# Three projection tiles begun with plain fp32 products of unsplit data, the early transfers timed anew, and a new order for the strips

## The chip, the cores and the metric

The kernel runs on one core of a Trainium2 chip. The metric is the device time of one execution in microseconds (us). The engines are TensorE (PE in the profile, its weight loads PEld), VectorE (DVE), ScalarE (ACT), GpSimd (POOL) and SyncE (SP). SP, ACT and POOL issue DMAs, each through a queue of its own.

## The reference

```python
x = A_x                                     # [1, 2048, 448]
g = sigmoid((x * gate_w).sum(-1, keepdims=True))
q, k, v = split(x @ wqkv)                   # 16 heads of 28
p = softmax(q @ k.T * 28 ** -0.5)           # 2048 x 2048 for each head
a = (p @ v) @ wo
b = gelu(layernorm(x) @ w1 + b1) @ w2 + b2  # 448 -> 1792 -> 448
return g * a + (1 - g) * b
```

Everything is fp32. The host only lays data out: x transposed with its 448 rows padded to four blocks of 128 (`xt`), and the weights cut into 128-wide tiles in the same four blocks.

## The kernel before, in words

**Split products.** A product of fp32 data is made of three or two products of split data. ACT rounds a raw tile to `fp32r` (the high part: `x_high`, `mixed_high`), DVE or POOL subtracts it from the raw tile (the low part: `x_low`, `mixed_low`), and PE adds high x high, high x low and low x high in one PSUM bank. A tile `QK(c, m)` is the 128 projection columns `m` of the 512 tokens of chunk `c`; `m` 0 to 6 covers queries and keys.

**Head.** The first three tiles, (0,0), (0,3) and (0,4), are made with the full 128-row array (L1011). SP loads weights and x chunk by chunk into eight raw slots (L984, L986); a slot is loaded again when both parts were made. Eight filler products (L991) stand before the first real one, four more between the first ones.

**Strips.** After that PE runs as four 32-row strips that work side by side on different matmuls (L549). A planner, `Strips.run`, is run while the program is written: it keeps a clock for each strip and for DVE, ACT, POOL and the DMA, and writes out the next matmul of the strip whose clock is lowest. So the order of PE is fixed; on the chip PE works it off in order. Three kinds of work share the strips: projections (`QK`, `Val`), the MLP (`Up`, `Down`), and the **row maxima** (L212): q x k scores of one head, 512 wide, in bank 6 or 7, whose row maximum DVE reduces (L214). There are 1024 of these and they are needed before the softmax of their query block. Wherever a row maximum is ready the planner takes it, except at the steps in the list `PASSES`, where it takes other work. What isn't made in the strips is left for attention. A piece of work handed from one strip to another goes through a semaphore that SP raises (L590), in SP's own order.

**Early transfers.** The first projections go to DRAM (`qk`) through ACT's queue (L304) and come back, head by head, through POOL's queue into `qd` (L196) and `kd` (L186); the first row maximum needs them. Chunk 3 of x comes through POOL's queue before that (L632). Weight tiles 2 and 6 take the places of tiles 0 and 3 and are asked for when these are done (`PLACE`, `done`).

**Attention.** A *turn* is four score tiles (`turn_of`, 12 matmuls, L1227), exponentials on ACT (L1233), and four products with v for the turn before (L1293, plain fp32). Two pairs of banks take the scores, the third pair is `spare`; the spare pair of one turn is the first pair of the next. While row maxima are left, `lone` puts one into bank 6 at the turn's start and one into bank `spare` at its end. Once none is left, the turns take a shorter form with all banks in a ring (L1260, L1261). At the end `finish_last` and `put` scale and project the last block, and SP stores it (L1096).

## Time and profile before

| | |
|---|---|
| time, median of 3 runs (lowest to highest) | 1023.41 us (1023.4 to 1024.1) |
| the profiled execution: its time, its span | 1024.39 us, 1022.6 us |
| PE busy | 1014.5 us, 99% |
| DVE busy | 747.3 us, 73% |
| ACT busy | 666.4 us, 65% |
| POOL busy | 359.6 us, 35% |
| row maxima: matmuls (L212), reductions (L214) | 1024 of 426 ns, 1024 of 689 ns |
| granted PE clock | 1.00 |

The profile is of one execution. Its own time is 1.8 us above its span; what lies between is start and end, and no query shows it. PE counts as busy whenever any strip works, so 99% doesn't say that four strips are full. The duration of a matmul includes its way through the array; what one costs is the distance between the starts of two that follow each other. The text after an arrow in a row names what ended the idle time before it.

### The profile page before, as it was taken

The numbers are of one execution on the slowest core, as the hardware profiler recorded it, in microseconds if no ns is written. First come the engines' busy times: TensorE is split into PE (matmuls) and PEld (weight loads), VectorE is DVE, ScalarE is ACT, GpSimd is POOL, SyncE is SP. The second block draws the span as 40 slices with busy tenths as digits, with TensorE's granted clock in tenths as the row PEclk, the third lists the DMA queues.
The fourth block names the chain that finished last, engine by engine and source line by source line (L and its number), as shares of the span: only waits on it lengthen the run. The fifth ranks groups of instructions, "written<-read, shape, count | busy, mean of one in ns | idle before, by whom it ended". The sixth has DMA issues, their size and how long they took to land.

```text
span 1022.6 us, 30999 instructions
## 1 busy us (share of the span) xinstructions
PE 1014.5 (99%) x13159; PEld 672.9 (66%) x13159; DVE 747.3 (73%) x1178; ACT 666.4 (65%) x1059; POOL 359.6 (35%) x376
## 2 busy tenths in 40 slices
PE   9999999999999999999999999999999999999998
PEld 7899999999999999944444444444444444464555
DVE  4899998999999999966666666656666666644111
ACT  5225365034043044189999999999999999969664
POOL 4558578626335034151011001400111223455324
PEclk9999999999999999999999999999999999999999
DMA  7688543211110014261000100310002101021121
GB/s 239 193 246 272 190 121 102 84 59 53 35 41 12 9 42 100 47 164 32 12 17 27 41 14 17 103 46 12 17 28 62 54 12 58 21 78 36 55 64 56
DMA packets 49666, 73.42 MB, mean 72 GB/s; under 512 B 13780, under 2 KB 30804, under 8 KB 48700
## 3 DMA queue, kind: packets, MB, share of 16 engines
q1 hardware_dynamic: 37096, 42.76, 14.5%
q0 software_dynamic: 4368, 14.39, 4.9%
q10 hardware_dynamic: 8064, 14.29, 3.9%
q8 instruction: 103, 1.69, 0.7%
q14 instruction: 35, 0.29, 0.1%
HBM read 51.98 MB, written 19.31 MB: 70 GB/s over the span
## 4 chain that ended last, share of the span: by engine, by line
PE 97%; DMA 2%; ACT 0%; DVE 0%; POOL 0%; SPq 0%; issue 0%
PE bk L549 35%; PE bk L1293 25%; PE bk L1227 17%; PE bk L212 15%; PE bk L1088 1%; DMA qk<-qo 1%; PE bk L1090 1%; PE bk L1089 1%; PE bk L1011 1%; DMA first<-in_xt 0%; ACT qo L300 0%; DMA kd<-qk 0%; POOL qd L196 0%; ACT xh L103 0%; PE bk L991 0%
## 5 line engine op out<-in xcount | busy, mean ns | idle before, releaser
L214 DVE TENSOR_REDUCE mx<-bk 128x1 f32<-128x512 f32 x1024 | 683.6, 689 | 174.4 <-PE bk L212 152.0
L1233 ACT ACTIVATE p<-bk 128x512 f32<-128x512 f32 (+1 forms) x693 | 462.4, 741 | 39.7 <-PE bk L1227 13.6
L212 PE MATMUL bk<-kd,qd 28*128 28x512 f32 x1024 | 435.0, 426 | 1.4 <-DMA kd<-qk 1.4
L212 PEld LDWEIGHTS bk<-kd,qd 28*128 28x128 f32 x1024 | 186.1, 182 | 201.9 <-DVE mx L214 180.4
L549 PE MATMUL bk<-yh,w1f 32*128 32x512 f32 x1568 | 182.4, 391 | 0.0
L549 PE MATMUL bk<-yl,w1f 32*128 32x512 f32 x784 | 159.3, 390 | 0.0
L549 PEld LDWEIGHTS bk<-yh,w1f 32*128 32x128 f32 x1568 | 151.2, 183 | 0.6
L549 PE MATMUL bk<-w2h,hh 32*128 32x448 f32 x896 | 140.3, 364 | 0.0
L549 PE MATMUL bk<-w2l,hh 32*128 32x448 f32 x896 | 139.8, 363 | 0.0
L1293 PE MATMUL bk<-p,vb 128*32 128x512 f32 x1024 | 136.2, 604 | 0.1
L1128 POOL TENSOR_TENSOR ot<-ob,rc 128x512 f32<-128x512 f32 x12 | 15.4, 1285 | 343.3 <-DMA rc<-rls 312.1
L1293 PE MATMUL bk<-p,va 128*32 128x512 f32 x1016 | 135.4, 605 | 0.0
L369 POOL TENSOR_TENSOR hl<-h,hh 128x512 fp32r<-128x512 f32 x56 | 72.0, 1296 | 124.5 <-ACT hh L361 51.7
L549 PEld LDWEIGHTS bk<-w2h,hh 32*128 32x128 f32 x896 | 105.5, 183 | 0.2
L549 PEld LDWEIGHTS bk<-w2l,hh 32*128 32x128 f32 x896 | 105.3, 183 | 0.1
L549 PEld LDWEIGHTS bk<-yl,w1f 32*128 32x128 f32 x784 | 103.8, 183 | 0.1
L1227 PE MATMUL bk<-yh,ka 29*128 29x512 f32 x508 | 92.6, 470 | 0.0
L549 PE MATMUL bk<-w2h,hl 32*128 32x448 f32 x896 | 87.2, 362 | 0.0
L1227 PE MATMUL bk<-yh,kb 29*128 29x512 f32 x512 | 86.4, 476 | 0.0
L360 ACT ACTIVATE h<-bk,b1s 128x512 f32<-128x512 f32 x56 | 38.2, 683 | 68.7 <-PE bk L549 50.8
L1227 PE MATMUL bk<-yh,la 28*128 28x512 f32 x508 | 79.5, 393 | 0.0
L1227 PE MATMUL bk<-yl,ka 28*128 28x512 f32 x508 | 78.8, 390 | 0.0
(147 smaller groups left out, 1610.0 us busy)
## 6 DMA issues: line engine op xcount, KB each, us to landing
qk<-qo ACTq DMA_DIRECT2D x28, 256.0 KB
raw<-in_xt SPq DMA_DIRECT2D x20, 256.0 KB
vs<-vt ACTq DMA_DIRECT2D x16, 256.0 KB
rc<-rls SPq DMA_DIRECT2D x60, 64.0 KB
bxr<-in_xk POOLq DMA_DIRECT2D x8, 448.0 KB, 5.4
yl<-qk SPq DMA_DIRECT2D x64, 56.0 KB
acc<-gbs SPq DMA_DIRECT2D x16, 224.0 KB
out_y<-acc SPq DMA_DIRECT2D x16, 224.0 KB
```

The costliest lines, as they stand in the source:

```text
L212: nc.tensor.matmul(ps, self.qd[n % 2][r, i * P:(i + 1) * P], self.kd[r, k * 512:(k + 1) * 512], start=True, stop=True)
L214: nc.vector.reduce_max(self.mx[n % 2][:, j, i, k:k + 1], ps, axis=AX)
L360: nc.scalar.activation(h, bk[:, self.bank], AF.Gelu_apprx_tanh, bias=b1s[:, f:f + 1])
L369: nc.gpsimd.tensor_sub(hl[f], h, hh[f].bitcast(F32))
L549: mm = nc.tensor.matmul(bk[:, x.bank, :n], a, b, start=x.first, stop=(len(x.rem) == 1 and m == len(ops) - 1), skip_group_check=True)
L1011: nc.tensor.matmul(bk[:, first[k].bank], w, v, start=(o == (k, hi, 0)), stop=(o == (k, by, 3)), skip_group_check=True)
L1088: nc.tensor.matmul(po, h, woh[:, g], start=(g == 0), stop=False, skip_group_check=True)
L1089: nc.tensor.matmul(po, h, wol[:, g], start=False, stop=False, skip_group_check=True)
L1128: nc.gpsimd.tensor_mul(ot[g][:, c * CH:(c + 1) * CH], ob, rc)
L1227: nc.tensor.matmul(bk[:, b], w[r, ks], q[r], start=(p == 0), stop=(p == 2), skip_group_check=True)
L1233: nc.scalar.activation(t[:, i:e], bk[:, b + i:b + e], AF.Exp, scale=SCALE)
L1293: nc.tensor.matmul(bk[32 * j:32 * j + 32, 7], vg[n // NC][:, k, 32 * j:32 * j + 32], prob[4 * b + j], start=(k == 0), stop=(k == NT - 1), ...
```

## The change

The head's order becomes x, x, then the three weight tiles, then x again, so that the first raw x block is there first. ACT's queue loads the first 128 rows of the three weight tiles a second time, unsplit, into a buffer that is idle then (`early_w`). PE takes the first of the four row blocks of the three tiles as three plain fp32 products of raw data (L992 in the new kernel) in place of nine split ones; the four fillers between products go, the eight ahead stay. The other products of the head stand in a new order. The evictions of the three tiles stand before the split of weight tile 1 on ACT.

Of the early transfers, weight tiles 2 and 6 get places in `yh` and `yl`, which are idle until the MLP, and are asked for at a fixed point; the first load of `qd` and `kd` is planned one microsecond later, and POOL's issue of a block of `kd` is planned with 2.05 us in place of 0.6.

`PASSES` goes from 15 to 91 steps, and the banks are tried in another order. In attention a row maximum comes from the other two strips when the first two have none ready, both may stand at the turn's start, and every 24th turn has a third one in bank `spare + 1`. The three small DVE steps that make the gate go from turn 2 to turns 21, 22 and 23, one each. The last output tile is scaled and stored in two halves, by SP and by ACT.

```diff
@@ -83,7 +83,6 @@
     lasting = [raws.tile([P, CH], F32, name=f"raw{i}") for i in range(4)]
     passing = [pr.tile([P, CH], F32, name=f"first{i}") for i in range(4)]
     wq, xh, xl = {}, {}, {}
-    PLACE = {2: 0, 6: 3}
 
     def four(r):
         return r.rearrange("p (a b) -> p a b", b=P)
@@ -238,10 +237,10 @@
     nc.vector.memset(rowmax.kd[:, 0:CH].bitcast(F32), 0.0)
 
 
-    PASSES = (1195, 1746, 2729, 2778, 2911, 3059, 4477, 5337, 6201, 6646, 6792, 6828, 6838, 7051, 7243)
+    PASSES = (2, 15, 55, 79, 86, 95, 105, 302, 435, 518, 533, 593, 618, 644, 975, 993, 1186, 1301, 1312, 1349,
...
     HOP = 0.51
     SCORED = 16.0
-    BANKS = (2, 1, 4, 5, 3, 0)
+    BANKS = (1, 2, 4, 0, 5, 3)
     RATE = 230.0
     RM = 0.65
     handoff = mybir.DependencyInfo(mybir.DependencyClass.Sync, mybir.DependencyReason.DATA)
@@ -648,7 +647,7 @@
 
         st.at(st.act + 0.1, rest)
 
-    def want_x(st, c, t):
+    def want_x(st, c, t, **kw):
         def then(slot, end):
             st.feed.back(slot, end)
             st.xs[c] = st.xs.get(c, 0) + 1
@@ -656,7 +655,7 @@
                 st.xready[c] = end
 
         st.feed.add(xt[t, :, c * CH:(c + 1) * CH], 256, lambda r: two(
-            st, lambda: x_high(c, t, r), lambda: x_low(c, t, r), "dve", 0.85, lambda end: then(r, end)))
+            st, lambda: x_high(c, t, r), lambda: x_low(c, t, r), "dve", 0.85, lambda end: then(r, end)), **kw)
 
     def want_wq(st, m, **kw):
         def then(slot, end):
@@ -664,7 +663,10 @@
             st.wready[m] = end
 
         def use(r):
-            wq[m] = pw.tile([P, 7, P], F32R, name=f"wq{PLACE.get(m, m)}")
+            if m in (2, 6):
+                wq[m] = (yh, yl)[m == 2][:, 0:2].rearrange("p a b -> p (a b)")[:, 0:7 * P].rearrange("p (a b) -> p a b", b=P)
+            else:
+                wq[m] = pw.tile([P, 7, P], F32R, name=f"wq{m}")
             two(st, lambda: mixed_high(wq[m], r), lambda: mixed_low(wq[m], r, m % 2), "pool", 1.6, lambda end: then(r, end))
 
         st.feed.add(wqk[m], 256, use, **kw)
@@ -800,13 +802,6 @@
         n = st.did[type(x), x.c]
         if isinstance(x, QK):
             st.qks.add((x.c, x.i))
-            for old, new in ((0, 2), (3, 6)):
-                if new not in wq and new not in st.asked and all((c, old) in st.qks for c in range(NC)):
-                    st.asked.add(new)
-                    want_wq(st, new)
-                    st.feed.queue.insert(0, st.feed.queue.pop())
-                    st.clock = max(st.clock, now)
-                    st.feed.pump()
             if x.i in (3, 4) and all((x.c, m) in st.qks for m in (3, 4)):
                 keys(st, x.c, now + 5.0)
             if not st.keyed and all((c, m) in st.qks for c in range(NC) for m in (3, 4)):
@@ -834,7 +829,7 @@
                     st.use("pool", st.clock, 0.55)
                     st.get(st.pool, 56)
             rowmax.load_block(c, nc.gpsimd)
-            st.use("pool", st.clock, 0.6)
+            st.use("pool", st.clock, 2.05)
             st.at(st.get(st.pool, 230) + 1.0, landed)
 
         def landed():
@@ -867,10 +862,12 @@
         st.wready.update({0: 0.0, 3: 0.0, 4: 0.0})
         st.late, st.later, st.shifted, st.unshifted = False, [], None, []
         st.xs, st.wvn, st.stats, st.lns, st.go, st.yn = {}, 0, 0, {}, {0}, {}
-        keys(st, 0, 4.0)
+        keys(st, 0, 5.0)
         for t in range(4):
-            want_x(st, 3, t)
+            want_x(st, 3, t, after=2.5)
         want_wq(st, 5, after=9.0)
+        for m in (2, 6):
+            want_wq(st, m, after=28.0)
         for t in range(4):
             want_wv(st, t, after=42.0)
         for f in range(NW):
@@ -919,10 +916,9 @@
         loads[0].dma_start(qh[n % 3][DH:P:32].bitcast(F32),
                           ms[n][0:16].rearrange("(j i) b x -> j (i b x)", j=4))
 
-    def gates():
-        nc.vector.tensor_scalar_add(gate, gate, 1.0)
-        nc.vector.reciprocal(gate, gate)
-        nc.vector.tensor_scalar(ngate, gate, -1.0, 1.0, op0=OP.mult, op1=OP.add)
+    gates = (lambda: nc.vector.tensor_scalar_add(gate, gate, 1.0),
+             lambda: nc.vector.reciprocal(gate, gate),
+             lambda: nc.vector.tensor_scalar(ngate, gate, -1.0, 1.0, op0=OP.mult, op1=OP.add))
 
     def early(st, now):
 
@@ -975,48 +971,56 @@
 
     loads = [nc.gpsimd]
     strips = Strips([])
-    load = [("wq", 0), ("x", 0, 0), ("wq", 3), ("wq", 4)] + [("x", 0, t) for t in range(1, 4)]
+    load = [("x", 0, 0), ("x", 0, 1), ("wq", 0), ("wq", 3), ("wq", 4), ("x", 0, 2), ("x", 0, 3)]
     load += [("x", 1, t) for t in range(4)] + [("wq", 1)] + [("x", 2, t) for t in range(4)]
     slots = passing + lasting
+    first = [QK(0, m) for m in (0, 3, 4)]
+    for k, x in enumerate(first):
+        x.bank = BANKS[k]
+    early_w = bxr[1][:, 0, 0:3 * P].rearrange("p (k a) -> p k a", a=P)
+    nc.scalar.dma_start(early_w[:, 0], wqk[0][:, 0])
+    nc.scalar.dma_start(early_w[:, 1:3], wqk[3:5].rearrange("m p t a -> p m t a")[:, :, 0])
+
+    def warm(n):
+        for _ in range(n):
+            nc.tensor.matmul(bk[:, 7], rowmax.kd[:, 0:P], rowmax.kd[:, 0:CH], start=True, stop=True, skip_group_check=True)
+
+    warm(8)
     for i, key in enumerate(load):
+        if i == 8:
+            for k, x in enumerate(first):
+                nc.tensor.matmul(bk[:, x.bank], early_w[:, k], slots[0], start=True, stop=False, skip_group_check=True)
         r = slots[i % 8]
         if key[0] == "wq":
             nc.sync.dma_start(four(r), wqk[key[1]])
         else:
             nc.sync.dma_start(r, xt[key[2], :, key[1] * CH:(key[1] + 1) * CH])
-        if 3 <= i < 15:
+        if 3 <= i < 14:
             head_split(i - 3)
-    def warm(n):
-        for _ in range(n):
-            nc.tensor.matmul(bk[:, 7], rowmax.kd[:, 0:P], rowmax.kd[:, 0:CH], start=True, stop=True, skip_group_check=True)
-
-    strips.feed.slots = slots[:4]
+    strips.dve = 1.2
     schedule_head(strips)
-    first = [QK(0, m) for m in (0, 3, 4)]
     parts = [x.full() for x in first]
-    hi, lo, by = range(3)
-    order = [(0, hi, 0), (0, by, 0), (0, lo, 0), 2, (1, hi, 0), (1, by, 0), 1, (1, lo, 0), (2, hi, 0), (2, by, 0), 1,
-             (0, hi, 1), (0, lo, 1), (1, hi, 1), (1, lo, 1), (2, hi, 1), (2, lo, 0), (2, lo, 1), (0, by, 1), (1, by, 1), (2, by, 1)]
-    for t in (2, 3):
-        order += [(k, p, t) for p in (hi, lo, by) for k in range(3) if p != lo or t < 3]
-    warm(8)
-    for k, x in enumerate(first):
-        x.bank = BANKS[k]
-    for o in order:
-        if isinstance(o, int):
-            warm(o)
-            continue
-        k, p, t = o
+    hi, by, lo = range(3)
+    order = [(0, hi, 1), (1, hi, 1), (0, lo, 1), (1, lo, 1), (2, hi, 1), (2, lo, 1)] + [(k, hi, 2) for k in range(3)]
+    order += [(0, by, 1), (0, by, 2)] + [(k, p, t) for p, t in ((lo, 2), (hi, 3), (lo, 3)) for k in range(3)]
+    order += [(1, by, 1), (1, by, 2), (2, by, 1), (2, by, 2)]
+    for k, p, t in order:
         w, v = parts[k][p][t]
-        nc.tensor.matmul(bk[:, first[k].bank], w, v, start=(o == (k, hi, 0)), stop=(o == (k, by, 3)), skip_group_check=True)
+        nc.tensor.matmul(bk[:, first[k].bank], w, v, start=False, stop=((k, p, t) == [o for o in order if o[0] == k][-1]),
+                         skip_group_check=True)
     for k, x in enumerate(first):
         x.close(strips, -0.25 * (2 - k))
-    strips.wready[1] = 1.0
-    for i in range(12, len(load)):
+    for i in range(3):
+        strips.feed.back(slots[i], 0.5 * i + 0.2)
+    for i in range(11, len(load)):
         head_split(i)
-        strips.use("act", 3.8, 0.65)
-        strips.use("dve", 4.6, 0.75)
-        strips.feed.back(slots[i % 8], strips.dve + 0.5)
+        strips.use("act", 0.5 * (i - 9), 0.65)
+        if i == 11:
+            strips.use("pool", strips.act + 0.1, 1.6)
+            strips.wready[1] = strips.pool + 0.2
+        else:
+            strips.use("dve", strips.act + 0.1, 0.75)
+        strips.feed.back(slots[i % 8], strips.wready[1] if i == 11 else strips.dve + 0.5)
     strips.xready[2] = strips.dve + 0.2
     for c, block in ((1, (3, 4, 0, 1)), (0, (1,)), (2, (3, 4)), (3, (3, 4)), (2, (0,)), (3, (0,))):
         strips.tiles += [QK(c, m) for m in block]
@@ -1043,7 +1047,7 @@
     woh = aw.tile([P, NG, D], F32R, name="woh")
     wol = aw.tile([P, NG, D], F32R, name="wol")
     ot = [aw.tile([P, S], F32, name=f"ot{g}") for g in range(NG - 1)]
-    agenda = {2: [gates]}
+    agenda = {21 + i: [fn] for i, fn in enumerate(gates)}
 
     def at(turn, fn):
         agenda.setdefault(turn, []).append(fn)
@@ -1092,8 +1096,10 @@
     def put(po, tt):
         c, i = divmod(tt, TPC)
         a = acc[c, i]
-        nc.vector.scalar_tensor_tensor(a, po, gate[:, tt:tt + 1], a, op0=OP.mult, op1=OP.add)
-        nc.sync.dma_start(out[tt], a)
+        parts = ((0, D),) if tt < NT - 1 else ((0, D // 2), (D // 2, D))
+        for k, (x, y) in enumerate(parts):
+            nc.vector.scalar_tensor_tensor(a[:, x:y], po[:, x:y], gate[:, tt:tt + 1], a[:, x:y], op0=OP.mult, op1=OP.add)
+            (nc.sync, nc.scalar)[k].dma_start(out[tt][:, x:y], a[:, x:y])
 
     def project(tt, b):
         po = bk[:, b, :D]
@@ -1216,6 +1222,7 @@
             else:
                 at(turn + 1, lambda n=n: rowmax.close(n))
                 at(turn + 2, lambda n=n: rowmax.store(n))
+        return s
 
     def score(x, p, b):
         n, k = divmod(x, 64)
@@ -1270,8 +1277,13 @@
         order = list(range(size))
         if turn in projected and size == 4 and sum(rowmax.cnt[s] for s in behind) < sum(rowmax.cnt[s] for s in ahead):
             ahead, behind, order = behind, ahead, [2, 3, 0, 1]
+        used = extra = None
         if rowmax.left() and turn not in projected:
-            lone(behind, 6, turn)
+            used = lone(behind, 6, turn)
+            if used is None:
+                used = lone(ahead, 6, turn)
+            if not any(rowmax.ready(x) and turn >= cold[x] for x in ahead if x != used):
+                extra = lone([x for x in behind if x != used], spare, turn)
         for step in range(4):
             for i in range(na):
                 if step < 3:
@@ -1283,8 +1295,10 @@
                 soften(u + order[0], 0, first, na)
         if nb:
             soften(u + order[2], 1, second, nb, 1)
-        if rowmax.left():
-            lone(ahead, spare, turn)
+        if rowmax.left() and extra is None:
+            s = lone([x for x in ahead if x != used], spare, turn)
+            if turn % 24 == 12:
+                lone([x for x in ahead if x not in (s, used)], spare + 1, turn)
         return size
 
     def batch(b, turn):
```

**PE, the head.** The names are the moving and the stationary operand: `kd` is zeros (fillers), `xh` and `xl` are the parts of x chunk 0, `wq` the split weight tiles 0, 3 and 4, `first` a raw slot, `bxr` the buffer of `early_w`. Before:

```order
L991 MATMUL bk<-kd 128x512 x8
L1011 MATMUL bk<-xh_182,wq_177 128x512
L1011 MATMUL bk<-xl_183,wq_177 128x512
L1011 MATMUL bk<-xh_182,wq_177 128x512
L991 MATMUL bk<-kd 128x512 x2
L1011 MATMUL bk<-xh_182,wq_187 128x512
L1011 MATMUL bk<-xl_183,wq_187 128x512
L991 MATMUL bk<-kd 128x512
L1011 MATMUL bk<-xh_182,wq_187 128x512
```

And in the changed kernel:

```order
L986 MATMUL bk<-kd 128x512 x8
L992 MATMUL bk<-first_134,bxr_150 128x512 x3
L1009 MATMUL bk<-xh_187,wq_195 128x512
L1009 MATMUL bk<-xh_187,wq_200 128x512
L1009 MATMUL bk<-xl_188,wq_195 128x512
L1009 MATMUL bk<-xl_188,wq_200 128x512
L1009 MATMUL bk<-xh_187,wq_205 128x512
L1009 MATMUL bk<-xl_188,wq_205 128x512
```

Three products of raw data stand where the split ones of the first row block stood, and no filler stands behind them; 24 split products follow (33 before).

**PE, a turn of attention with a third row maximum.** `kd` x `qd` are row maxima, `yh`, `yl`, `ka`, `la` the parts of the scores, `p` and `va` the product with v. Every such turn before:

```order
L212 MATMUL bk<-kd,qd_153 128x512
L1227 MATMUL bk<-yh,ka 128x512 x2
L1227 MATMUL bk<-yh,la 128x512 x2
L1227 MATMUL bk<-yh,ka 128x512 x2
L1227 MATMUL bk<-yl,ka 128x512 x2
L1227 MATMUL bk<-yh,la 128x512 x2
L1227 MATMUL bk<-yl,ka 128x512 x2
L212 MATMUL bk<-kd,qd_153 128x512
L1293 MATMUL bk<-p_10099,va 32x512 x2
L1293 MATMUL bk<-p_10103,va 32x512 x2
```

And one of the eight turns of the changed kernel that have three:

```order
L211 MATMUL bk<-kd,qd_153 128x512
L1234 MATMUL bk<-yh,ka 128x512 x2
L1234 MATMUL bk<-yh,la 128x512 x2
L1234 MATMUL bk<-yh,ka 128x512 x2
L1234 MATMUL bk<-yl,ka 128x512 x2
L1234 MATMUL bk<-yh,la 128x512 x2
L1234 MATMUL bk<-yl,ka 128x512 x2
L211 MATMUL bk<-kd,qd_153 128x512
L211 MATMUL bk<-kd,qd_152 128x512
L1307 MATMUL bk<-p_10060,va 32x512 x2
L1307 MATMUL bk<-p_10064,va 32x512 x2
```

The third stands behind the second, ahead of the product with v, and writes bank `spare + 1`.

**PE, near the end of the row maxima.** Two turns of the changed kernel have both row maxima at their start, where before none has:

```order
L211 MATMUL bk<-kd,qd_153 128x512 x2
L1234 MATMUL bk<-yh,kb 128x512 x2
L1234 MATMUL bk<-yh,lb 128x512 x2
L1234 MATMUL bk<-yh,kb 128x512 x2
L1234 MATMUL bk<-yl,kb 128x512 x2
L1234 MATMUL bk<-yh,lb 128x512 x2
L1234 MATMUL bk<-yl,kb 128x512 x2
```

The second of the two writes bank `spare` at the start of its turn and not at the end. Counted over the whole order, 570 row maxima stand ahead of the first product with v before, and 557 now; the last row maximum stands in turn 229 before and in turn 231 now.

1 line of the change is left out of this document (added).

## The prediction

> **What bounds the kernel now.** I read the page's chain of waits first, then busy time by stage: head, three stretches of the strips, attention.
>
> ```profile
> PE 97%; DMA 2%; ACT 0%; DVE 0%; POOL 0%; SPq 0%; issue 0%
> ```
> ```profile
> 0.00:14.45 14.45, 12.42 (x45) 9.27 (x45) 7.16 (x13) 9.21 (x14) 6.96 (x22) 1.00 0.78 261
> 14.45:200.00 185.55, 183.68 (x3168) 177.82 (x3171) 165.29 (x274) 73.06 (x142) 123.84 (x147) 1.00 0.57 178
> 200.00:400.00 200.00, 200.00 (x3522) 192.65 (x3518) 197.41 (x311) 64.38 (x104) 75.08 (x60) 1.00 0.13 39
> 400.00:436.60 36.60, 36.60 (x676) 35.46 (x671) 36.21 (x57) 7.91 (x14) 8.06 (x7) 1.00 0.33 71
> 436.60:938.00 501.40, 501.30 (x5110) 212.90 (x5110) 330.29 (x504) 461.66 (x694) 110.03 (x110) 1.00 0.15 42
> ```
>
> After the stretch and its length come PE, weight loads, DVE, ACT, POOL. PE is the bound throughout: what makes it wait, or gives it one step more, is paid in full. From 200 to 436.6 us DVE is full too (233.6 of 236.6 us); in attention it has a third of its time free.
>
> **The head.** It ends with the first strip matmul (32 rows) at 14.45.
>
> ```profile
> 1.63 3.62 PE L991 MATMUL bk<-kd 128*128 128x512 f32 x8 [1.63 <-DVE kd L238]
> 5.08 0.41 PE L1011 MATMUL bk<-xh,wq 128*128 128x512 f32 x1
> 8.67 1.77 PE L1011 MATMUL bk<-xh,wq 128*128 128x512 f32 x7
> 14.45 0.50 PE L549 MATMUL bk<-xh,wq 32*128 32x512 f32 x3
> 6.18 0.33 SPq L986 DMA_DIRECT2D first<-in_xt  x1
> 11.52 1.88 DVE L106 TENSOR_TENSOR xl<-first,xh 128x512 fp32r<-128x512 f32 x3
> ```
>
> Seven split products take 1.77 us, the last one 0.41 of it: 0.23 us each. From 5.08 to 14.45 are 9.37 us; 33 products and four fillers at 0.23 are 8.5, so 0.9 was waiting for splits. Now come three plain fp32 products. None of this shape is in the trace; the nearest are the products with v, where four side by side take from 602.36 to 603.35, 0.99 us (rows below). I take 0.9 each, 2.7 in all, then 24 split products at 0.23, 5.5: strips from about 13.3. That is **1.1 us** won. Both raw pieces must have landed by 5.08. The old first product at 5.08 needed two loads as large and their rounding besides, so they should have; if not, the gain can go to nothing; without any wait and with 0.85 a product it is 1.3.
>
> The Trainium skill (TensorE: Matmul & The Clock Gate, What you observe) says that the clock doubles around 4 us into sustained matmul work, give or take 0.5. Here eight fillers take 3.62 us and the distances after 5.08 are the short ones, so the trace agrees to within that margin. By the page the first raw product could run partly at half speed, and the sum would be 0.3 us worse.
>
> A price is hidden here: x(1,1) goes into the slot of x(0,0), which PE now reads until 7.8, so SP issues it 1.6 us later than 6.18. In the old order x chunk 1 was split by 13.40, 1 us ahead of the strips; in the head DVE works 7.16 and ACT 9.21 of 14.45 us, and I take it as covered. Uncovered it costs the 1.1.
>
> **The first row maximum.**
>
> ```profile
> 16.70 0.82 ACTq L304 DMA_DIRECT2D qk<-qo  x2
> 17.12 0.64 ACT L103 ACTIVATE xh<-raw 128x512 fp32r<-128x512 f32 x1
> 23.95 2.04 POOL L196 DMA_DIRECT2D qd<-qk  x4 [6.87 <-DMA qk<-qo]
> 25.98 2.00 POOL L186 DMA_DIRECT2D kd<-qk  x4
> 26.85 0.38 PE L549 MATMUL bk<-xh,wq 32*128 32x512 f32 x1
> 28.60 0.97 PE L212 MATMUL bk<-kd,qd 28*128 28x512 f32 x2 [1.37 <-DMA kd<-qk]
> 70.17 0.47 PE L549 MATMUL bk<-xh,wq 32*128 32x512 f32 x1 [0.50 <-SPq L590]
> ```
>
> PE reaches the first row maximum at 26.9 and stands until 28.60 for `kd`, then 0.4 for the next piece: 2.0 us. `kd` follows POOL's first issue at 23.95 by 4.65, and that waits for the stores that ACT issues at 16.70. Now the evictions stand earlier on ACT: the last begins at 13.4, 0.4 behind the last product. It, one split more and three conversions at 0.64 each, less the 0.42 by which the stores went out ahead of the fourth conversion, give 16.2; I allow up to 16.7. POOL's loads of x chunk 3, which ran beside them, now stand behind the split of weight tile 1, 1.4 us later, so the stores should be through no later: `kd` at 27.6 to 28.6. PE wants it later in its order: 229 strip products are ahead, 209 before, 20 x 0.0575 = 1.15, and about 1 us goes on the split of weight tile 1 (an estimate: evictions and split, 3 us from 13.3, cover most of the tiles ahead): 26.9 - 1.1 + 1.15 + 1 = 28.0. I take 0.4 of waiting, **1.6 us** won; the bounds are 2.0 won and 1 lost. The 0.5 at 70.17, SP raising a hand-over behind small DMA issues, should stay.
>
> **The strips.** 13 row maxima fewer stand in them (557, was 570).
>
> ```profile
> L214 DVE TENSOR_REDUCE mx<-bk 128x1 f32<-128x512 f32 x570 | 371.3, 688 | 16.8 <-PE bk L212 11.3 <-PE bk L549 2.0
> ```
>
> If PE alone paces, each is a quarter of 0.23 us: 0.75 in all. If DVE paces, each is 371.3 / 570 = 0.65: 8.5 us. Nine of the 13 fall where DVE is full: 9 x 0.65 + 4 x 0.06 = 6.1. How far the new `PASSES` fill PE's strips no row shows. I take **4.0 us** won, nearer to DVE's price, since DVE has 1.3% free there.
>
> **Attention.** First a turn before, then PE rows of two turns in the short form.
>
> ```profile
> 601.22 0.49 PE L212 MATMUL bk<-kd,qd 28*128 28x512 f32 x1
> 601.80 0.62 PE L1227 MATMUL bk<-yl,kb 28*128 28x512 f32 x4
> 602.03 0.39 PE L212 MATMUL bk<-kd,qd 28*128 28x512 f32 x1
> 602.36 1.06 PE L1293 MATMUL bk<-p,vb 128*32 128x512 f32 x8
> 603.35 0.50 PE L212 MATMUL bk<-kd,qd 28*128 28x512 f32 x1
> 603.36 0.51 PE L1227 MATMUL bk<-yh,kb 29*128 29x512 f32 x3
> 604.48 1.06 PE L1293 MATMUL bk<-p,vb 128*32 128x512 f32 x8
> 601.75 1.43 DVE L214 TENSOR_REDUCE mx<-bk 128x1 f32<-128x512 f32 x2 [0.69 <-PE bk L212]
> 603.89 0.69 DVE L214 TENSOR_REDUCE mx<-bk 128x1 f32<-128x512 f32 x1 [0.71 <-PE bk L212]
> 601.10 0.59 ACT L1233 ACTIVATE p<-bk 128x512 f32<-128x512 f32 x1
> 601.57 0.61 ACT L1233 ACTIVATE p<-bk 128x512 f32<-128x512 f32 x1
> ```
> ```profile
> 941.72 1.07 PE L1293 MATMUL bk<-p,vb 128*32 128x512 f32 x8
> 943.62 1.07 PE L1293 MATMUL bk<-p,vb 128*32 128x512 f32 x8
> ```
>
> A long turn is 2.12 us (602.36 to 604.48), a short one 1.90. Row maxima last two turns longer now: 2 x 0.22 = **0.4 lost**.
>
> The third row maximum of a turn writes `spare + 1`, where the next turn's second score goes at 603.36. DVE ends the second reduction at 603.18; a third, 0.6 to 0.69 behind it, ends at about 603.8. How such a wait looks is seen at turn 2, where the gate's three steps hold DVE up:
>
> ```profile
> 442.93 1.00 DVE L923 TENSOR_SCALAR gate<-gate 128x16 f32<-128x16 f32 x1
> 444.24 0.18 DVE L925 TENSOR_SCALAR ngate<-gate 128x16 f32<-128x16 f32 x1
> 444.34 1.27 DVE L214 TENSOR_REDUCE mx<-bk 128x1 f32<-128x512 f32 x2
> 445.27 0.49 PE L212 MATMUL bk<-kd,qd 28*128 28x512 f32 x1
> 445.67 0.51 PE L1227 MATMUL bk<-yh,ka 29*128 29x512 f32 x4
> ```
>
> The reduction ends at 445.61, the scores start at 445.67, 0.4 after the row maximum that they go with in other turns. So a third costs 603.86 - 603.36 = 0.5, behind it stand the rest of the turn and its product with v, and PE has no slack to win it back: eight turns, **4.0 lost** (0 if the wait hides, 5.8 at a whole reduction and release each). In the two turns with both at the start, the second needs bank `spare` at 601.2, where ACT reads until 601.69: 2 x 0.5 = **1.0 lost** (0 to 1.2). The gate's steps, spread over three turns, fit DVE's 0.7 of idle time: **0.4 won**. The halved last tile I put at nothing, 0.2 either way: the stores ahead of it fill the queue.
>
> Sum: -1.1 - 1.6 - 4.0 + 0.4 + 4.0 + 1.0 - 0.4 = -1.7. The profiled execution took 1024.39 (span 1022.6 and 1.8 around it), so 1022.7; the median before is 0.98 below it, which gives **1021.7 us**.
>
> **The rivals.**
> - *The third reduction hides* (DVE has 0.7 us free per turn): no 5.0 lost, 1016.7. Against it stands turn 2, where PE waited. 0.13.
> - *DVE paces the strips* at 0.65 for each of the 13: 4.5 more won, 1017.2. For it, DVE's 98.7%; against it, the first 186 us, where it has 20 us free. 0.10.
> - *`kd` comes back late again*, since the later loads of chunk 3 still share the DMA engines with the stores: the 1.6 stay lost, 1023.3. 0.15.
> - *The new order doesn't pack the strips*: only 0.75 is won there, 1025.0. 0.12.
> - *The new order makes PE wait for DVE at banks 6 and 7*. Before, the strips hold hardly a wait on it; an order with less slack makes PE stand for a reduction of 0.65 wherever two come too close. Ten such places cost 6.5: 1028.2, slower; it decides from six. 0.08.
>
> **How the numbers follow.** The forecast has 0.42, its own range 1020.2 to 1023.3. About 0.2% (2.0 us) is what a measurement can tell from no change. The forecast lies 0.35 us inside that, so 0.17 of its 0.42 counts as faster; with the first two rivals faster has 0.40. Slower has 0.08 and a quarter of the fourth rival, 0.11; the same has 0.49. The range 1017.0 to 1024.4 leaves out the last rival, half of the fourth and half of the first: 0.2.
>
> **What would show it.** The first 32-row matmul at 13.3; the first row maximum near 28.4 with under 0.6 of waiting for `kd`; the strips' end at about 430, not 436.6; eight long turns of about 2.6 us and two more near the end; the 0.4 us at 445.67 gone. Wrong it is if the eight turns stay at 2.12, if the strips win under 2 or over 6 us, or if the head ends after 14.

## The result, and the profile after

The changed kernel took 1029.85 us (median of 6 runs, 1028.6 to 1031.38) beside 1023.86 us (6 runs, 1023.4 to 1026.65) for the kernel before: a ratio of 1.0055, 95% interval 1.0041 to 1.0069. It is slower; 1021.7 was predicted, with a range up to 1024.4. The profiled execution took 1030.52 us, its span is 1028.7. Four executions of the experiments below (one of the thirds alone, one with `kd` through POOL, two with stores and gates alone) took 1097 to 1900 us in a slow state; the ratios leave them out, and without them these three medians are 1026.84, 1031.90 and 1023.19 us.

First the chain of waits of the kernel after by engine, then its stages (stretch, length, busy time and count of PE, weight loads, DVE, ACT, POOL, then granted PE clock, DMA share, GB/s), cut where those of before were cut: at the first strip product and at the strips' end.

```profile
PE 95%; DMA 3%; DVE 1%; issue 0%; ACT 0%; SPq 0%; DVEq 0%; ACTq 0%; POOLq 0%
```
```profile
0.00:14.80 14.80, 12.42 (x38) 7.56 (x38) 7.57 (x13) 9.16 (x14) 5.96 (x20) 1.00 0.73 243
14.80:200.00 185.20, 181.81 (x3118) 173.12 (x3121) 160.67 (x266) 72.95 (x142) 122.50 (x146) 0.99 0.57 180
200.00:400.00 200.00, 200.00 (x3559) 193.73 (x3555) 195.18 (x307) 64.33 (x103) 78.06 (x63) 1.00 0.11 35
400.00:437.90 37.90, 36.60 (x675) 35.38 (x667) 35.79 (x57) 8.00 (x15) 8.25 (x7) 1.00 0.42 93
437.90:938.00 500.10, 500.03 (x5075) 213.46 (x5076) 332.11 (x509) 458.23 (x688) 110.15 (x109) 1.00 0.16 42
```

PE's share of the chain fell from 97% to 95%, and DMA and DVE took the two points. In the first stretch of the strips PE now stands idle 3.4 us (185.20 less 181.81; before 1.9) and its clock is 0.99; in the last it stands 1.3 us (before none). Between 200 and 400 us the new order did what it was to do: PE issues 3559 products there, 3522 before, and DVE is busy 2.2 us less.

The stages by their ends, in us (first product with v as the end of the strips):

| | before | after | change | predicted |
|---|---|---|---|---|
| first strip product | 14.45 | 14.80 | +0.35 | -1.1 |
| from there to the first product with v | 423.4 | 424.4 | +1.0 | -5.6 |
| from there to the end of the span | 584.7 | 589.5 | +4.8 | +5.0 |
| span | 1022.6 | 1028.7 | +6.1 | -1.7 |

So attention went as predicted, and what is missing, 8.05 us (0.35 + 1.0 + 1.1 + 5.6), lies in front of it. Four places hold most of it. A wait is given below as the distance between the starts of two matmuls of PE; the idle time in a row's brackets is shorter, since the matmul before is still running.

**The head.** PE rows of the kernel after, and POOL's last split.

```profile
4.93 3.02 PE L992 MATMUL bk<-first,bxr 128*128 128x512 f32 x6
11.40 0.61 PE L1009 MATMUL bk<-xh,wq 128*128 128x512 f32 x2
12.76 0.50 PE L1009 MATMUL bk<-xh,wq 128*128 128x512 f32 x1 [0.75 <-POOL wq L96]
14.80 0.50 PE L548 MATMUL bk<-xh,wq 32*128 32x512 f32 x3
```
```profile
11.92 0.79 POOL L96 TENSOR_TENSOR wq<-raw,wq 64x128 fp32r<-64x128 f32 x1
```

The three raw products are six records that start at 4.93 to 7.37, the last three 0.43 apart, which is 0.86 a product: as estimated. But the 24 split products behind them (from 7.80 to 14.80) take 7.0 us, not 5.5. One of them waits for POOL's last split of a weight tile, which ends at 12.71; this wait is 0.9 of the 1.5.

**The first row maximum.** Rows of ACT and POOL of the kernel after, the third store in its chain of waits (issue, time to landing), PE, then the clock in short stretches.

```profile
14.46 1.08 ACT L299 ACTIVATE qo<-bk 128x512 f32<-128x512 f32 x2 [0.33 <-PE bk L1009]
16.77 1.92 ACT L102 ACTIVATE xh<-raw 128x512 fp32r<-128x512 f32 x3 [0.19 <-DMA raw<-in_xt]
18.05 2.47 ACTq L303 DMA_DIRECT2D qk<-qo  x3
```
```profile
18.02 2.38 POOL L631 DMA_DIRECT2D first<-in_xt  x4
28.46 1.00 POOL L185 DMA_DIRECT2D kd<-qk  x2 [2.36 <-DMA qk<-qo]
```
```profile
18.93 9.02 DMA qk<-qo
```
```profile
29.26 0.50 PE L211 MATMUL bk<-kd,qd 28*128 28x512 f32 x1
31.36 0.50 PE L211 MATMUL bk<-kd,qd 28*128 28x512 f32 x1 [1.61 <-DMA kd<-qk]
31.96 1.05 PE L548 MATMUL bk<-xh,wq 32*128 32x512 f32 x5
```
```profile
29.00:31.89 2.89, 1.28 (x18) 0.68 (x14) 0.69 (x1) 0.00 (x0) 1.01 (x2) 1.00 0.87 254
31.89:35.30 3.41, 3.41 (x36) 2.74 (x33) 1.88 (x3) 1.12 (x2) 1.40 (x3) 0.50 0.21 65
35.30:45.00 9.70, 9.70 (x170) 9.07 (x166) 9.28 (x15) 1.20 (x2) 4.54 (x9) 1.00 0.74 244
```

ACT issues the stores only at 18.05. Ahead of them in its order stand the split of weight tile 1 and three conversions, as the prediction's sum had it, and they wait only 0.2 us for loads; what is late is the last eviction, which starts at 14.95 and not at 13.4 because the head ends late. At 18.02 POOL issues the four loads of x chunk 3, and the third store takes 9.02 us to land. POOL's last two loads of `kd` wait 2.36 us for it, and PE stands 2.10 us between 29.26 and 31.36. Then comes what no step of the prediction had: the granted clock is 0.50 for 3.41 us, PE issues 36 products in them and not some 60, and by half of the 3.41 us 1.7 more are gone.

**DVE beside POOL, 117 to 121 us.** One row of each engine of the kernel after, then the four subtractions of this line after and before (shortest, middle and longest in ns).

```profile
117.74 2.81 DVE L763 TENSOR_TENSOR raw<-raw,lnr 128x512 f32<-128x512 f32 x1
```
```profile
117.45 2.54 POOL L785 TENSOR_TENSOR yl<-raw,yh 128x512 fp32r<-128x512 f32 x2
```
```profile
121.21 0.50 PE L211 MATMUL bk<-kd,qd 28*128 28x512 f32 x1 [1.01 <-DVE mx L213]
```
```profile
L763 DVE TENSOR_TENSOR raw<-raw,lnr x4: 754/900/2807, 108.3 to 117.7; 128x512 f32<-128x512 f32 x4
L761 DVE TENSOR_TENSOR raw<-raw,lnr x4: 682/938/1632, 105.1 to 109.4; 128x512 f32<-128x512 f32 x4
```

The last subtraction takes 2.81 us; the longest before took 1.63. The reduction behind it ends late, and PE's products start 1.37 us apart (119.83, 121.21).

**The last group of `kd`, 400 to 415 us.** SP's queue and PE of the kernel after, then SP's last load of this group before.

```profile
400.40 0.31 SPq L179 DMA_DIRECT2D kd<-qk  x1
...
406.38 0.82 SPq L179 DMA_DIRECT2D kd<-qk  x2
```
```profile
414.59 0.47 PE L211 MATMUL bk<-kd,qd 28*128 28x512 f32 x1 [1.30 <-DMA kd<-qk]
```
```profile
397.90 0.31 SPq L180 DMA_DIRECT2D kd<-qk  x1
```

PE stands 1.65 us (412.94 to 414.59) for the last of these loads, issued at 406.38 to 407.2 between loads for attention. Before, the four were issued by 398 us and PE did not wait.

**Attention.** PE rows of a turn with a third row maximum in the kernel after, DVE's row, and the starts of the products with v around the two turns with both maxima at the start.

```profile
462.62 1.07 PE L1307 MATMUL bk<-p,va 128*32 128x512 f32 x8
464.43 0.68 PE L211 MATMUL bk<-kd,qd 28*128 28x512 f32 x2
465.04 1.07 PE L1307 MATMUL bk<-p,va 128*32 128x512 f32 x8
467.39 0.64 PE L1307 MATMUL bk<-p,va 128*32 128x512 f32 x4
```
```profile
464.15 2.06 DVE L213 TENSOR_REDUCE mx<-bk 128x1 f32<-128x512 f32 x3 [0.66 <-PE bk L211]
```
```profile
940.01 1.07 PE L1307 MATMUL bk<-p,vb 128*32 128x512 f32 x8
942.63 1.07 PE L1307 MATMUL bk<-p,vb 128*32 128x512 f32 x8
945.27 1.07 PE L1307 MATMUL bk<-p,vb 128*32 128x512 f32 x8
947.39 1.06 PE L1307 MATMUL bk<-p,vb 128*32 128x512 f32 x8
```

The turn takes 2.42 us and the next 2.35, where two plain ones take 4.24: 0.53 for a third. So it is at six of the eight thirds; at two the next turn is plain, 0.30: 3.8 us in all, with DVE's three reductions in a row as foreseen. The two turns with both at the start take 2.62 and 2.64.

### The profile page after: what moved, and what is told of

Read it like the earlier page. It is cut to its first block, busy times and chain, and to the rows that moved or that the text cites. A ratio compares the mean times of both kernels' runs of the same rounds, so it can differ in the third digit from the quotient of the medians.

```text
span 1028.7 us, 30979 instructions
## 1 busy us (share of the span) xinstructions
PE 1017.1 (99%) x13152; PEld 670.9 (65%) x13152; DVE 747.9 (73%) x1179; ACT 666.1 (65%) x1049; POOL 360.7 (35%) x376
## 4 chain that ended last, share of the span: by engine, by line
PE 95%; DMA 3%; DVE 1%; issue 0%; ACT 0%; SPq 0%; DVEq 0%; ACTq 0%; POOLq 0%
PE bk L548 33%; PE bk L1307 25%; PE bk L1234 17%; PE bk L211 15%; DMA qk<-qo 2%; PE bk L1092 1%; PE bk L1094 1%; PE bk L1093 1%; DMA kd<-qk 1%; DMA raw<-in_xt 0%; DMA first<-in_xt 0%; PE bk L986 0%; PE bk L992 0%; DVE raw L763 0%; DVE mx L213 0%
## 5 line engine op out<-in xcount | busy, mean ns | idle before, releaser
L548 PEld LDWEIGHTS bk<-w2h,hh 32*128 32x128 f32 x896 | 100.0, 183 | 0.6
L548 PEld LDWEIGHTS bk<-w2l,hh 32*128 32x128 f32 x896 | 99.8, 183 | 0.1
```

Source lines behind the costliest of these rows:

```text
L548: mm = nc.tensor.matmul(bk[:, x.bank, :n], a, b, start=x.first, stop=(len(x.rem) == 1 and m == len(ops) - 1), skip_group_check=True)
```

## The experiments

The ratios below are to runs of the kernel before on the same chip in the same session (medians 1023.83 to 1024.31), with their 95% intervals; a difference between two kernels is the difference of their ratios, times 1024, and uncertain by some 1.3 us, by 1.7 to 2.0 where the change itself is one of the two; below that the profile's places decide and not the time alone. Places in the strips are read from one profile each.

### The thirds and the new rule for single row maxima alone, in the kernel before

```diff
-            lone(behind, 6, turn)
+            used = lone(behind, 6, turn)
+            if used is None:
+                used = lone(ahead, 6, turn)
+            if not any(rowmax.ready(x) and turn >= cold[x] for x in ahead if x != used):
+                extra = lone([x for x in behind if x != used], spare, turn)
...
-        if rowmax.left():
-            lone(ahead, spare, turn)
+        if rowmax.left() and extra is None:
+            s = lone([x for x in ahead if x != used], spare, turn)
+            if turn % 24 == 12:
+                lone([x for x in ahead if x not in (s, used)], spare + 1, turn)
```

> The kernel before with the changed kernel's rule for row maxima in attention alone (a third one every 24th turn, both at a turn's start when the other strips have none). Its order has seven turns with a third one and one with two at the start, and the last row maximum in turn 223 (229 before). Theory (a third reduction makes the next turn's score wait 0.5 us): seven pairs of turns longer by 0.5 each, one start 0.5, six turns in the short form 1.3 won: +2.7 us, 1026.6. Rival (the reductions hide in DVE's idle time, and what attention lost came with the new strips): -1.3 us.

Measured: 1026.92 us, ratio 1.0025 (1.0014 to 1.0036). Seven turns hold a third, each 2.42 or 2.43 us long, and four of them are followed by one of 2.33 to 2.35: 0.30 to 0.53 for each. The price of a third is shown: it doesn't hide.

### The new head alone, in the kernel before, with either order of the loads

The first kernel has the head of the change whole; in the second the weights of tile 0 are loaded first, as before.

```diff
-    load = [("x", 0, 0), ("x", 0, 1), ("wq", 0), ("wq", 3), ("wq", 4), ("x", 0, 2), ("x", 0, 3)]
+    load = [("wq", 0), ("x", 0, 0), ("wq", 3), ("wq", 4)] + [("x", 0, t) for t in range(1, 4)]
```

> The kernel before with the changed kernel's head alone: two x blocks loaded ahead of the weight tiles, three plain fp32 products, the new order of the other 24. Theory (with the weights loaded later, POOL's split of the third weight tile ends at about 12.7 and the head waits for it): first 32-row matmul at 14.8, not earlier than before (14.45); the whole run 0 to 2 us slower by later stores of the first tiles. Rival (the raw products themselves are slow): the same 14.8, but with no wait for POOL, and again 14.8 in the run that loads the weights first.

> The kernel before with the three plain fp32 products, but with its own order of loads (weight tile, x, two weight tiles, x). Theory: POOL is done with the third weight tile by 10, nothing waits at the head's end, first 32-row matmul at 13.4 to 13.7 (14.45 before). The first row maximum still waits for kd, which comes no earlier, so of the 0.8 to 1.0 us at most half reaches the end: 0 to -0.6 us. Rival (the raw products cost the time): 14.8 and slower than before.

Measured: 1026.71 us, ratio 1.0025 (1.0014 to 1.0037), strips from 14.83; and 1026.61 us, 1.0030 (1.0017 to 1.0043), strips from 15.52, which is a miss. A row of PE of the first, and one of the second.

```profile
12.78 0.50 PE L1013 MATMUL bk<-xh,wq 128*128 128x512 f32 x1 [0.73 <-POOL wq L97]
```
```profile
10.31 0.73 PE L1013 MATMUL bk<-xl,wq 128*128 128x512 f32 x2 [1.01 <-DVE xl L106]
```

With x first, the weight tiles' splits on POOL end late; with the weights first, x(0,1) comes fifth and its low part is late. The raw products save PE work in front of a chain of loads and splits that is no shorter. In the ten profiles with the new head as it is in the change the strips start at 14.72 to 15.05, in the four with the old head at 14.45 to 15.06: that the new head is not faster is shown, that it is 0.35 slower is not. The first kernel waits 2.52 us for `kd`, and its clock too falls, from 29.39 us on:

```profile
29.39:36.20 6.81, 6.46 (x57) 5.24 (x61) 3.17 (x5) 1.60 (x3) 1.66 (x3) 0.50 0.68 206
```

### The stores of the head's three tiles directly behind their evictions

```diff
+            if self in first:
+                nc.scalar.dma_start(rows, t)
+                st.at(st.act + 0.3, lambda: st.get(st.clock, 256), act=0.35)
+                return
             st.at(st.act + 0.3, lambda: (nc.scalar.dma_start(rows, t), st.get(st.clock, 256)), act=0.35)
```

> The changed kernel with the stores of the first three tiles issued on ACT directly behind their evictions, ahead of the split of weight tile 1 and of x chunk 2. Nothing else moves. Theory (the third store goes out at 18.9 together with the loads of x chunk 3 and lands at 28.4, so kd is late, PE stands 2.1 us and then runs 3.4 us at half clock): the stores are issued by 16.8 and landed by about 24, no wait of over 0.5 us at the first row maxima, no half clock there: -3.0 to -3.8 us. Rival (the loads of chunk 3 hold the stores and kd up wherever they are issued): the wait stays over 1.5 us, the time within 1 us.

Measured: 1026.57 us, ratio 1.0028 (1.0019 to 1.0038): 2.8 us less than the change. The third store on ACT's queue and the first two row maxima on PE:

```profile
16.10 0.33 ACTq L304 DMA_DIRECT2D qk<-qo  x1
```
```profile
29.08 0.38 PE L211 MATMUL bk<-kd,qd 28*128 28x512 f32 x1
29.53 0.50 PE L211 MATMUL bk<-kd,qd 28*128 28x512 f32 x1
```

The wait of 2.10 is 0.45, and the clock stays at 1.00. When the stores are issued decides `kd`; it was 18.05 in the change, where 16.2 to 16.7 had been worked out. Most kernels below hold this edit too; their expectations say so.

### PE kept busy through the wait

```diff
+            if sum(rowmax.cnt) == 1:
+                for _ in range(6):
+                    nc.tensor.matmul(bk[:, b], wq[0][:, 0], xh[0][:, 0], start=True, stop=True, skip_group_check=True)
             ends = rowmax.one(s, bk[:, b])
```

> The kernel after with six products of old data (128x512, some 0.21 us each, their result is overwritten) ahead of the second row maximum, the one for which PE waits 2.10 us for kd. They hold no load back. Theory (the granted clock falls to half behind the wait because PE stands idle for too long, and costs some 1.7 us beyond the wait): the second row maximum still starts at about 31.4 us, but its products behind it run 0.21 us apart and not 0.42, 1029.85 - 1.7 = 1028.1 us. Rival (the clock falls there for another reason, as the load on the chip): half clock from about 32 us again, 1029.9 us.

Measured: 1027.93 us, ratio 1.0039 (1.0025 to 1.0053): 1.6 us less than the change. PE rows, and the clock in the stretch that answers to the one of 0.50 above:

```profile
30.10 1.67 PE L567 MATMUL bk<-xh,wq 128*128 128x512 f32 x6
31.70 0.50 PE L211 MATMUL bk<-kd,qd 28*128 28x512 f32 x1
```
```profile
32.00:35.40 3.40, 3.40 (x62) 3.05 (x57) 2.69 (x5) 1.59 (x3) 1.35 (x2) 1.00 0.33 128
```

The wait is as long as it was, 1.96 us, but PE works in it, the clock stays, and 62 products go through in place of 36. The difference in time would not tell it by itself, and a single profile without a fall does not either: the mean granted clock is 0.998 or less in every profile with a fall and 0.999 or 1.00 in every other, and by that three of the change's six executions have one and one of these five has one too. What speaks for the idle PE as the cause is the count over all kernels (last part): where this wait is short, the clock hardly ever falls.

### Fewer thirds

```diff
-            if turn % 24 == 12:
+            if turn in (12, 36, 60, 132, 156):
```

> The kernel after, its head tiles' stores behind their evictions (as in e4_after_stores), and the third row maximum given in five turns (12, 36, 60, 132, 156) and not at every 24th; the order then has one turn with both maxima at its start and not two, and its last row maximum one turn later. Theory (each third reduction costs 0.5 us of its own turn, and the strips keep what they gain): against e4_after_stores three thirds fewer, -1.5, one turn with both at the start fewer, -0.5, one more long turn, +0.2: 1026.6 - 1.8 = 1024.8 us, attention 587.5 against 589.3. Rival (the attention is longer because there are 13 more row maxima left for it, wherever they stand): the count is the same, 589.3 and 1026.6 us.

Measured: 1025.73 us, ratio 1.0010 (1.0001 to 1.0018), 1.8 us less than with eight thirds; attention 587.6 us. Both as the theory had it: the price follows the count. By the theory 0.5 of it is not a third but one turn fewer with both at the start.

### The last group of `kd`: through POOL's queue, or planned later

```diff
-                        rowmax.load_k(n, j)
+                        rowmax.load_k(n, j, nc.gpsimd if n == 2 else nc.sync)
```
```diff
-                        self.hot[j] = self.get(self.clock + 0.6, 224) + 1.0
+                        self.hot[j] = self.get(self.clock + 0.6, 224) + (4.0 if n == 2 else 1.0)
```

> The kernel after with the head tiles' stores behind their evictions, and the four loads of kd's last group issued by POOL and not by SP, where they stand behind the loads of la, yl and qd. Theory (the 1.3 us for which PE waits at 410 us in e4_after_stores, 1.65 us at 413 us in the kernel after, are the time that these loads stand in SP's queue): the wait is gone, strips 418.9 and not 420.2, 1025.3 us. Rival (the loads are late because all DMA engines are 0.74 busy there, or because the planner gives the third maximum of a group too late): the wait stays, 1026.6 us.

> The kernel after with the head tiles' stores behind their evictions, and in the planner the four loads of kd's last group counted as landed 3 us later than it counts them (no load is moved in its queue; row maxima that need them are given later, other strip work earlier). Theory (they take 6.5 to 8 us from issue to landing while the loads of la, yl and qd share the DMA engines, which are 0.8 to 0.96 busy there; the planner counts some 2 us, so it gives the row maxima too early): PE's wait at about 410 us falls from 1.33 to under 0.4 us, three row maxima pass to the attention, 1026.6 - 1.3 + 0.3 = 1025.6 us. Rival (there is no other work left to give PE there): the wait stays or becomes one for DVE, 1026.6 us.

Through POOL: 1031.98 us, ratio 1.0073 (1.0061 to 1.0085). POOL issues the first of the four only at 398.28, behind its own work, and PE stands 3.87 us in front of a row maximum, with the clock at half from 405.37 on; the row names no cause, and that it is these loads is read from their times.

```profile
398.28 1.08 POOL L179 DMA_DIRECT2D kd<-qk  x2
```
```profile
406.21 0.76 PE L211 MATMUL bk<-kd,qd 28*128 28x512 f32 x1 [3.51 <-issue]
```

Neither theory had a longer wait. From issue to landing these loads take 6.5 to 8.2 us here, so SP's queue alone was not the cause. Planned later: 1026.33 us, ratio 1.0019 (1.0010 to 1.0028), 0.9 less by the ratios, but the strips are no shorter (420.1 us, 420.2 without the edit). PE's wait for `kd` is gone, and 0.67 us for another load stands there:

```profile
411.43 0.50 PE L552 MATMUL bk<-yh,ka 29*128 29x512 f32 x2 [0.24 <-DMA yh<-ms]
```

The rival was nearer: at the strips' end there is little other work to give PE. That loads this slow were planned as fast is shown by the wait that went; what it is worth to plan them right was not shown.

### The subtractions of tile 0 by POOL, with the planner told and not told

In the first kernel the planner's account follows (`st.use("pool", ...)`), so it draws the strips up anew behind 100 us; in the second only the engine is changed, and PE's order is word for word the same.

```diff
-            nc.vector.tensor_sub(r, r, lnr[c][:, 0])
+            nc.gpsimd.tensor_sub(r, r, lnr[c][:, 0])
```

> The kernel after with the head tiles' stores behind their evictions, and the four subtractions raw - lnr of tile 0 done by POOL and not by DVE (they stand beside POOL's subtractions: the last of them took 2.8 us, from 0.3 us behind the start of one POOL instruction to 0.5 us behind the end of the next, and PE waits 1.4 us for the reduction queued behind it). The planner then draws up the strips behind 100 us anew: 593 row maxima stand ahead of the first value product of the attention and not 557, the thirds are five and not eight, and the last row maximum is in turn 214 and not 231. Theory (DVE stands still while POOL has what both need): no wait of PE for DVE near 115 us. Sum against e4_after_stores: strips 420.2 + 36 x 0.23 - 1.4 = 427.1, attention 589.3 - 3 x 0.5 - 17 x 0.22 = 584.1: 1028.4 us (1027 to 1029.5). Rival for the wait (the subtraction is long whatever runs beside it, or the reduction would be late anyway): a wait of 1 us or more stays there.

> The kernel after with the head tiles' stores behind their evictions, and the four subtractions raw - lnr of tile 0 given to POOL and not to DVE with the planner's account left as it was, so that PE's and ACT's order is the same, word for word, and DVE's but for the four. Theory (PE's 1.4 us at 115 us are DVE standing still beside POOL): the wait is gone, 1026.57 - 1.4 = 1025.2 us. Rival (POOL, now 1.3 us more for each of the four, hands yl over too late, and PE waits there instead; or another reduction is late): 1026.6 us or more.

Planner told: 1041.46 us, ratio 1.0158 (1.0143 to 1.0173). The old wait is gone, but the strips take 441.4 us and not the 427.1 of the sum. They hold 36 row maxima more than in the kernel with the order kept, and are 23.6 us longer: 0.66 us for each. That is near DVE's 0.65 and far from PE's 0.23, but it isn't shown to be DVE's price: 10.2 us of these strips ran at half clock, by which some 5 of the 23.6 are lost. At 126 and at 181 us the profile shows row maxima that follow each other, PE standing for each reduction, and there the clock falls. Not told: 1025.64 us, ratio 1.0015 (1.0006 to 1.0024), 1.3 us less than without the edit, strips 417.8 us and no wait of PE left between 100 and 250 us. DVE's reductions there now follow each other with nothing between:

```profile
115.30 3.26 DVE L213 TENSOR_REDUCE mx<-bk 128x1 f32<-128x512 f32 x5 [1.17 <-PE bk L211]
```

That PE waited for this subtraction on DVE is shown, since nothing but its engine was changed. That POOL beside it made it so long rests on the overlaps in the traces (last part).

### Two products of the head moved to its end

```diff
+    late = [(2, hi, 3), (2, lo, 3)]
+    order = [o for o in order if o not in late] + late
     for k, p, t in order:
```

> The kernel after with the head tiles' stores behind their evictions, and in the head the two products of the third tile's fourth row block that use its high part (high x high, high x low) moved to the end of PE's order, behind the low x high products of tiles 1 and 2. Nothing else moves. Theory (PE's order, not the loads, ends the head late: at 12.68 it waits 1.14 us for POOL's last split while seven products behind it could run): the seven fill the wait, strips start at 13.6 and not 14.72, 1026.57 - 1.1 = 1025.5 us, or up to 0.6 more if kd's loads do not come earlier with it. Rival (the loads and splits pace the head): a wait stands at another product, strips from 14.5, 1026.4 us.

Measured: 1026.80 us, ratio 1.0019 (1.0010 to 1.0028), 0.9 us less by the ratios; but its profile has the strips from 14.76, not 13.6. No wait for POOL is left; here the raw products were slow:

```profile
5.21 3.82 PE L996 MATMUL bk<-first,bxr 128*128 128x512 f32 x6
```

The six records start at 5.21, 6.06, 6.91, 7.58, 8.01 and 8.44: the first at half clock, 0.85 apart, the last at full, 0.43. The granted clock rose at 7.38 us here, and in other kernels with this head at 4.58 (the change), 5.06, 5.50, 6.22 and 7.76. So the head's end also hangs on when in the execution the clock comes up. In the two kernels below that have this order the strips start at 14.51 (clock from 4.64 us) and 14.57 (from 6.22), some 0.3 ahead of 14.83. The theory's 1.1 has fallen.

### All parts put right, in the kernel after and in the kernel before

In the kernel after, with the head of before, or with all that paid:

> The kernel after with the head of before (split products, the weights of tile 0 loaded first), the head tiles' stores behind their evictions, five thirds, and kd's last group issued by POOL. Theory: strips 419 against 423.4 of before, a start at 14.45 as before, attention +3.2 (five thirds 2.5, one turn with both at the start 0.5, three more long turns 0.6, gates -0.4): 1023.8 - 4.4 + 3.2 = 1022.6 us (1021.6 to 1023.3). Rival (what the shorter strips gain is given back in the attention one for one, whatever the count of thirds): 1023.8 or more.

> The kernel after with all that is put right in it: stores behind the evictions, the two products of the head at the end, the four subtractions by POOL in the same order, and the third in five turns. Sum by the parts as measured or expected: e4_after_stores 1026.57, five thirds -0.84, head -1.1, subtraction -1.4: 1023.2 us (1022.6 to 1024.2), so within the error of before. Rival (the parts overlap in kd's path and the strips): 1025 us or more.

The first took 1029.79 us, ratio 1.0054 (1.0042 to 1.0066): POOL's late `kd` loads cost it 3.74 us and the clock again. The second took 1024.18 us, ratio 0.9994 (0.9984 to 1.0004): no different from before.

Three causes taken away together, but with the planner told of the subtractions:

> The kernel after with the head tiles' stores behind their evictions and three of the causes taken away together: the subtractions of tile 0 by POOL, the four loads of kd's last group planned 4 us later, and the third only in the turns 12, 36, 60, 132, 156. The planner leaves 588 row maxima ahead of the first value product and not 557, and two thirds, no turn with both maxima at its start, the last row maximum in turn 218. Sum against e4_after_stores: strips 420.2 + 31 x 0.23 - 1.4 - 1.3 = 424.6, attention 589.3 - 6 x 0.5 - 2 x 0.5 - 13 x 0.22 = 582.4: 1024.1 us (1022.5 to 1025). Rival (each stall taken away opens another of its size): 1026.5 or more.

It took 1038.86 us, ratio 1.0145 (1.0131 to 1.0158); its strips take 438.0 us, and again the clock falls, for 6.8 us, where row maxima follow each other.

In the kernel before, the stores and the gates alone, and these with the new head:

```diff
-    agenda = {2: [gates]}
+    agenda = {21 + i: [fn] for i, fn in enumerate(gates)}
```

> The kernel before with the two parts that paid by themselves: the stores of the three head tiles directly behind their evictions, and the three gate instructions spread over turns 21 to 23. Theory: PE's wait for kd of 1.75 us at about 29 us falls below 0.8, and the attention's turn 3 from 2.52 to 2.12 us: 1023.8 - 1.0 to 1.8 - 0.4 = 1021.6 to 1022.4. Rival (the third piece of kd is held up by the transfers around it, not by when it is issued): only the 0.4, 1023.4 us.

> The kernel before with what paid by itself: the head of the change (raw products, its loads) with the two products at the end as in s13_head_order, the three stores directly behind their evictions, and the gate's steps in the turns 21 to 23. Theory: strips from 13.7 and not 14.45, no wait for kd, 0.4 of the gate: r7_before_stores_gates had 1023.4 against 1024.3, less 0.75: 1022.6 us (1022.0 to 1023.3). Rival (the earlier strips only meet kd earlier and wait there): 1023.4 us.

The first took 1023.41 us, ratio 0.9992 (0.9983 to 1.0001). Its wait for `kd` of 1.75 us is gone, yet less than 1.0 of it shows; in its profile the strips start at 15.06, though the head is that of before, and a hand-over by SP takes 1.28 us. The second took 1022.61 us, ratio 0.9983 (0.9974 to 0.9992): it beats both kernels, before by 1.7 us (0.8 to 2.7). It keeps the old `PASSES` and the old rule for single row maxima. That 1022.6 was expected is luck in part: the theory had the strips start at 13.7, and they start at 14.51, no earlier than before. The 0.9 us between the two kernels is within the uncertainty, so no gain of the head is shown. What ends its head late is DVE's split, for 0.41 us:

```profile
12.47 0.73 PE L1018 MATMUL bk<-xl,wq 128*128 128x512 f32 x2 [0.41 <-DVE xl L106]
14.51 0.50 PE L553 MATMUL bk<-xh,wq 32*128 32x512 f32 x3
```

## Why the prediction was wrong, step by step

- **The head, -1.1: wrong, +0.35.** The price of a raw product was right (0.86, estimated 0.9). The failed step is "24 split products at 0.23, 5.5": it let the splits keep up. With x loaded first the weight tiles come later and POOL's six split instructions end at 12.71; with the other load order DVE's are late; with the product order changed some 0.3 is won. The head is a chain of loads and splits, and PE's work was not its bound. That PE already stood 0.9 us for splits in the old head was in the prediction's own sum, and it was counted as won.
- **The first row maximum, -1.6: wrong.** The stores that ACT was to issue at 16.2 to 16.7 went out at 18.05, beside the loads of chunk 3. The split and the three conversions ahead of them were in the sum; its start failed, "the last begins at 13.4", which was 14.95. So 1.55 of the 1.85 us come from the head. "The stores should be through no later" failed too: the third took 9.02 us to land. The rival "`kd` comes back late again" named the place and the sharing; its price, "the 1.6 stay lost", was too low, since the wait grew to 2.10 and the clock took 1.7 more. The prediction took a wait to cost its own length. Against a wait of 0.4 this is 3.4 us in the profiled execution.
- **The strips, -4.0: the size right, but not the result.** Without their waits of over 0.5 us the strips of before take 420.8 us (423.4 less 1.75 and 0.89). Those of the change take 416.0 (424.4 less 2.10, 0.56 and 0.99 at SP's hand-overs, 1.37, 1.65, and 1.7 of the clock): 4.8 less; by the profile of the change with the stores moved it is 3.9. Over 13 row maxima that is 0.3 to 0.4 each, between the two prices, so neither is shown. What failed is that this gain was summed without asking which new waits a new order brings: 1.37 for DVE, 1.65 for `kd`, 0.7 more at SP, 3.7 in all. The first two come back, at 1.2 to 1.5 us, in each profile with this order and none of the edits made against them. The 0.7 at SP is not shown to come from the order: with the strips of before, word for word, the run of the thirds alone has 1.58 us there and the profile before 0.89.
- **The rival "the new order makes PE wait for DVE"** (1028.2, 0.08) came near in time by chance. There was one such wait, not ten, and not at two reductions too close but at a subtraction beside POOL.
- **Attention, +5.0: right, +4.8.** The eight thirds 3.8 (4.0), the two turns with both at the start 1.0 (1.0); the turn of 2.52 with the gate's steps is gone (0.4). Fewer thirds gave less by as much. The price of 0.5 came from one row at turn 2 where such a wait could be seen.

Sum: 1.45 at the head, 3.4 at `kd`, 3.7 of new waits, less 0.8 that the strips gained beyond 4.0, is 7.75 of the 8.05 us missing in front of attention, by one profile of each kernel; attention came out 0.2 better than forecast.

## What to carry to other kernels

When PE's work in front of a chain of loads and splits is made less, ask for each product left when its operand is ready: the chain's end and not PE's sum gives the time. A new order of a full engine brings new waits at places that had none, so look for engines that share something, and for loads that are planned faster than they land. A wait on PE can cost more than its length when the clock falls behind it, and then filler work inside the wait may pay.
